# A convolution's kernels loaded with time on the partitions in 64 byte pieces, and the first stage of their transform made from two float16 parts

## The chip, the core and the metric

One core of a Trainium2 chip runs the whole program. The metric is the device time of one execution in microseconds (us). Before the change its median over three runs is 2721.65 us (2719.81 to 2725.82). The engines are named as the profile names them: PE (TensorE, with PEld for its weight loads), ACT (ScalarE), DVE (VectorE), POOL (GpSimd), SP (SyncE, which here only issues DMAs). A queue of an engine runs in the order in which the built program wrote it: an instruction that waits holds back all that stand behind it on that engine.

## What is computed

Four layers follow each other on x of 2048 positions by 640 channels: attention with 32 heads of 20 channels, a convolution over time (S4D), the same attention and the same convolution again. Cut to what matters:

```python
x = x + attention(layernorm(x), wqkv, wo)
x = x + s4d(layernorm(x), ...)        # and both once more, same weights

def s4d(u):
    dt = exp(log_dt); A = -exp(log_A_real) + 1j*A_imag; C = (C_real + 1j*C_imag)*dt[:, None]
    K = 2*einsum("dn,dnl->dl", C, exp((A*dt[:, None])[:, :, None]*arange(L))).real   # 640 x 2048
    y = irfft(rfft(u, 2L) * rfft(K, 2L))[:L]
    return y + u*D_skip
```

K holds one kernel of 2048 taps for each of the 640 channels. Both convolutions use the same K, so the program makes K once, transforms it once, and keeps its transform in HBM.

## The kernel before, in words

**The attention.** For each of 8 groups of heads and 4 blocks of 512 queries the kernel walks over 16 tiles of keys (`attention`, from line 394). `scores` (L824) fills a PSUM tile S, ACT takes its exponential into `pt` (2048 activations of 128 by 1024), and `values` (L841) adds up `pa`, two PSUM tiles with one buffer each. At the end of a block DVE takes `pa` out (`COPY oc<-pa`, then an add of the second tile), and only then can the next block's first `values` write it again. The division by the sum of the exponentials goes by HBM: POOL writes the sums (`dn<-oc`), reads them back (`dr<-dn`), DVE inverts `dr`, POOL writes and spreads it (`db<-dn`), and DVE multiplies one block later. While the attention runs, the object `Plan` estimates when each engine is free, and that decides which pieces of other work stand between the attention's instructions. In this part DVE, ACT, POOL and SP are tied to the order in which the instructions are written down.

**The kernels K.** `kgen` (L182) makes K during the first attention: DVE builds tables of powers, PE contracts them (`contract`, L315), DVE takes the result out as `ko`, and POOL writes `ko` to the HBM tensor `kd`, 640 channels by 2048 taps. Its last piece is written during the last group of heads. Then `end_jobs` calls `prefetch` (L972), which loads `wo`, splits it on POOL, and loads `x` again for the residual.

**The output projection.** `out_proj` (L1092) runs 16 steps `s`. Each takes a tile `otl` of the attention's output from HBM, splits it into `oh` (ACT) and `ol` (DVE), makes 30 matmuls of 128 by 320 into two PSUM tiles `po` (L1098, L1104), and DVE adds them to x. Behind it `ln_u` (L1013) makes the next layernorm: statistics on DVE, `u` on DVE, the float16 part `uh` on ACT and the rest `ul` on POOL.

**The transform of K.** `ktransform` (L1029) is written into step 2 of the first `out_proj`, and the scheduler mixes both. For each of five sets of 128 channels `unit_load` (L1044) does this:

- It loads `kl` from `kd`, with channels on partitions and 8 KB in a row, and adds the skip weight to tap 0 (one DVE instruction of 128 by 1).
- 16 float32 transposes on PE (L1053) turn it into `ktr`, time on partitions. ACT and DVE take them out of PSUM.
- Stage one: 32 float32 matmuls of 128 by 128 with the table `e1` (L1061), into 8 PSUM tiles `pkx` (two buffers), which ACT and DVE take out in turn into `kx`.
- Then 8 steps `q` of a pipeline: four transposes (L1070), ACT takes them out (`kxt`), one float32 matmul of 128 by 512 with `f2` (L1078), two shuffles on DVE into `kn`, one sign product on ACT, and after every second step two DMAs of 512 KB to the HBM tensors `kha` and `khb`.

**The convolution.** `ssm` (L1128) follows. Its `stage1` (L1155) makes, from `uh` and `ul` and a float16 table `e1s` in two parts, three float16 matmuls of 128 by 128 for each one that a float32 form would need (L1163).

Of the kernel before, what the change touches and what calls it, by code (L numbers as in the profile page):

```python
# [11 lines left out]
F32 = mybir.dt.float32  # L12
F32R = mybir.dt.float32r
F16 = mybir.dt.float16
# [70 lines left out]
def mha_s4d_kernel(ctx, tc, x_in, wqkv, wo, lar, aim, cr, ci, ldt, dsk,  # L85
# [23 lines left out]
    def pst(pool, *a, **k):  # L109
        return ps_[pool].tile(*a, **k)  # L110
# [21 lines left out]
    warm = cp.tile([P, 1], F32, name="warm")  # L132
    ve.memset(flag, 0.0)
# [48 lines left out]
    def kgen():  # L182
# [180 lines left out]
        while pend or busy():  # L363
            yield "wait"
        kw2.__exit__(None, None, None)
# [606 lines left out]
    def prefetch(x, rest):  # L972
# [40 lines left out]
    def ln_u(x, i0, n, mvrs, uh, ul, pool):  # L1013
        mv, rs = mvrs
        for i in range(n):
            s = i0 + i
            u = pool.tile([P, D], F32, name="u")
            ve.tensor_scalar(u, x[:, s, :], mv[:, i, 0:1], rs[:, i:i + 1], ALU.subtract, ALU.mult)
            se.copy(uh[:, s, :], u)
            (ve if s == NI - 1 else ge).tensor_sub(ul[:, s, :], u, uh[:, s, :])  # L1020
# [8 lines left out]
    def ktransform():  # L1029
# [4 lines left out]
        e1 = c1.tile([P, NI, 2, P], F32, name="e1")  # L1034
        sy.dma_start(e1, c_e1.rearrange("p (i r k) -> p i r k", i=NI, r=2))
# [5 lines left out]
        skip = c1.tile([P, NCT], F32, name="skip")  # L1041
        sy.dma_start(skip, dsk)

        def unit_load(b):  # L1044
            kl = c1.tile([P, L], F32, name="kl")
            sy.dma_start(kl, kd[b * P:b * P + P, :])
            ve.tensor_add(kl[:, 0:1], kl[:, 0:1], skip[:, b:b + 1])
            kt = c1.tile([P, NI, P], F32, name="ktr")
            klv = kl.rearrange("d (p i) -> d i p", i=NI)
            for i4 in range(4):  # L1050
                pt = pst("T", [P, 4, P], F32, tag="T", name="pkt")
                for i in range(4):
                    te.transpose(pt[:, i, :], klv[:, 4 * i4 + i, :], ident)  # L1053
                (se.copy if i4 % 2 else ve.tensor_copy)(kt[:, 4 * i4:4 * i4 + 4, :], pt)
                yield
            x1 = c1.tile([P, 32, NI // 2, 16], F32, name="kx1")
            for i2 in range(NI // 2):
                ps = pst("X", [P, 2, 2, P], F32, tag="X", name="pkx")
                for r in range(2):
                    for i in range(2):  # L1060
                        te.matmul(ps[:, r, i, :], e1[:, 2 * i2 + i, r, :], kt[:, 2 * i2 + i, :],  # L1061
                                  start=True, stop=True)
                (ve.tensor_copy if i2 % 2 else se.copy)(by_channel(x1, i2), ps.rearrange("p r i (g c) -> p (r i) g c", c=4))
                yield
            prev = None
            for q in range(9):
                if q < 8:
# [4 lines left out]
                    se.copy(xt, pt.rearrange("p g k -> p (g k)"))  # L1072
                if prev is not None:
                    g0 = b * 32 + 4 * (q - 1)
                    if q % 2:
                        kn = [c1.tile([P, 2, 512], F32, name=f"kn{s}") for s in range(2)]
# [270 lines left out]
    def seq(x, general):  # L1347

        stats = None
        for n in range(0, len(parts), 2):  # L1350
            with ExitStack() as c:
# [16 lines left out]
                with ExitStack() as c2:  # L1368
                    up2 = c2.enter_context(tc.tile_pool(name="up2", bufs=2))

                    def ln(i0, m):
                        ln_u(x, i0, m, ln_stats(lambda i: x[:, i0 + i, :], m), uh, ul, up2)
# [3 lines left out]
                    else:  # L1376
                        if n == 0:
                            filler[:] = ktransform(), 0.0, False
# [91 lines left out]
```

## Time and profile before

| What | Time |
|---|---|
| median of three runs | 2721.65 us |
| the profiled execution | 2718.84 us |
| its span, from its first to its last instruction | 2717.1 us |
| granted TensorE clock over the span | 0.991 |
| PE busy | 2534.4 us (93%) |
| ACT busy | 2337.4 us (86%) |
| DVE busy | 1477.0 us (54%) |
| POOL busy | 852.6 us (31%) |
| the first attention's last `pa` taken out of PSUM | 1100.95 us after the start |
| first L1104 matmul of `out_proj` in layer 1 | 1102.4 us |
| first transpose of `ktransform` | 1140.96 us |
| last matmul of `out_proj` in layer 1 | 1282.24 us |
| last `pkf` matmuls of `ktransform` begin | 1277.44 us |

The profile gives busy time for each engine, the idle time before a group of instructions with what ended it, and on request a timeline of any stretch and the sums of a stretch. An average over the span says little here, since in the attention ACT never rests and in the output projection PE hardly does. A stage has to be read by its own rows.

### The profile page before, as it was taken

Reading aid. Unit: us, or ns where it says so; the run is one execution under the profiler, and the core shown is the slowest. Engines: PE = TensorE matmul, PEld = TensorE weight load, DVE = VectorE, ACT = ScalarE, POOL = GpSimd, SP = SyncE. Lnnn points to the kernel's source line nnn. Section 1 sums busy time; section 2 is a strip of 40 time slices with the busy share of each in tenths; the row PEclk is TensorE's granted clock in tenths of the full one; section 3 lists DMA queues with packets and bytes.
Section 4 is the critical chain, followed back from the end, with each engine's and each line's share of the span. In section 5 each row is a group of like instructions: output and inputs, shape, how many; then the busy total and the mean of one; then the engine's idle time right before and its main releaser. Section 6 shows DMA issues by size and latency. Waiting matters only on the chain.

```text
span 2717.1 us, 115609 instructions
## 1 busy us (share of the span) xinstructions
PE 2534.4 (93%) x50944; PEld 1445.2 (53%) x50944; DVE 1477.0 (54%) x3292; ACT 2337.4 (86%) x2762; POOL 852.6 (31%) x1282
## 2 busy tenths in 40 slices
PE   7899999999999988999999999899999998888998
PEld 3445444444444433777886445444445443335988
DVE  7777877778856970577776332232232220003865
ACT  7899999999999999455655899899999999997464
POOL 1132333333333343301670122222223223222376
PEclk9999999999999999999999999999999999999999
DMA  6522222232222232455542111111121112112365
GB/s 214 174 62 75 63 77 64 73 75 61 65 51 59 51 112 87 145 210 194 178 142 67 45 52 52 50 53 46 46 66 35 50 36 61 41 38 80 110 191 161
DMA packets 183153, 238.55 MB, mean 88 GB/s; under 512 B 42737, under 2 KB 128241, under 8 KB 180849
## 3 DMA queue, kind: packets, MB, share of 16 engines
q1 hardware_dynamic: 146304, 184.48, 21.0%
q0 software_dynamic: 36336, 46.59, 7.2%
q8 instruction: 402, 6.59, 1.0%
q14 instruction: 111, 0.90, 0.1%
HBM read 154.90 MB, written 76.03 MB: 85 GB/s over the span
## 4 chain that ended last, share of the span: by engine, by line
ACT 49%; PE 30%; issue 9%; DVE 7%; DMA 4%; POOL 1%; SPq 0%; ACTq 0%; DVEq 0%; POOLq 0%
ACT pt L77 47%; PE pa L841 5%; PE S L824 3%; PE psv L1198 3%; PE po L1104 3%; PE psy L1208 2%; PE m L578 2%; PE psx L1186 2%; PE psx L1163 2%; PE po L1098 1%; PE pst L1173 1%; PE pkf L1078 1%; DMA kop<-ks 1%; PE pv L544 1%; PE pq L730 1%
## 5 line engine op out<-in xcount | busy, mean ns | idle before, releaser
L77 ACT ACTIVATE pt<-S 128x1024 f32<-128x1024 f32 x2048 | 1922.9, 1037 | 46.7 <-PE S L824 37.1
L841 PE MATMUL pa<-pt,V 64*32 64x512 f32 x16384 | 1101.0, 590 | 0.9 <-DVE oc L77 0.8
L824 PE MATMUL S<-qop,kop 61*32 61x512 f16 x16384 | 880.4, 381 | 125.4 <-ACT pt L77 105.1
L824 PEld LDWEIGHTS <-kop 61*32 61x32 f16 x16384 | 375.1, 89 | 784.1 <-issue 660.0
L841 PEld LDWEIGHTS pa<-pt,V 64*32 64x32 f32 x16384 | 315.0, 106 | 69.9 <-DVE oc L77 6.6
L77 POOL DMA_DIRECT2D dn<-oc x256 | 126.7, 501 | 700.9 <-DVE oc L77 644.7
L77 DVE COPY oc<-pa 128x512 f32<-128x512 f32 x64 | 44.2, 690 | 312.1 <-PE pa L841 307.2
L77 DVE TENSOR_SCALAR qc<-m 128x512 f32<-128x512 f32 (+1 forms) x68 | 46.9, 689 | 296.4 <-PE m L578 296.4
L77 POOL DMA_DIRECT2D db<-dn x256 | 130.0, 513 | 111.6 <-DMA dn<-dr 107.7
L578 PE MATMUL m<-xh,wh 64*32 64x512 f16 x2560 | 146.7, 379 | 1.4 <-DVE qc L77 1.4
L578 PE MATMUL m<-xh,wl 64*32 64x512 f16 x2560 | 147.3, 378 | 0.0
L578 PE MATMUL m<-xl,wh 64*32 64x512 f16 x2560 | 145.5, 377 | 0.0
L77 POOL DMA_DIRECT2D ot<-oc x256 | 130.2, 516 | 12.7 <-issue 8.3
L578 PEld LDWEIGHTS <-wh 64*32 64x32 f16 x5120 | 92.5, 94 | 74.1 <-issue 32.6
L1191 POOL TENSOR_TENSOR t<-t,kb 128x512 f32<-128x512 f32 x80 | 102.0, 1276 | 72.3 <-DVE t L77 58.2
L77 ACT COPY xt<-pst 128x1024 f16<-128x1024 f16 x80 | 81.5, 1022 | 47.6 <-PE pst L1173 47.5
L77 POOL DMA_DIRECT2D dn<-dr x64 | 35.8, 559 | 257.5 <-DVE dr L77 237.1
L544 PEld LDWEIGHTS <-xh 128*128 128x128 f16 x960 | 79.6, 98 | 50.9 <-issue 35.6
L77 DVE TENSOR_TENSOR kb<-ktab 128x512 f32<-128x512 f32 x160 | 106.3, 682 | 0.0
L77 DVE TENSOR_SCALAR V<-m 128x160 f32<-128x160 f32 x64 | 20.7, 324 | 156.3 <-PE m L544 156.3
L77 DVE TENSOR_SCALAR dr<-dr 128x16 f32<-128x16 f32 x64 | 11.0, 171 | 171.8 <-DMA dr<-dn 171.6
L1020 POOL TENSOR_TENSOR ul<-u,uh 128x640 f16<-128x640 f32 x30 | 46.1, 1555 | 177.7 <-ACT uh L77 177.7
(269 smaller groups left out, 4045.7 us busy)
## 6 DMA issues: line engine op xcount, KB each, us to landing
ka<-kha SPq DMA_DIRECT2D x80, 256.0 KB
kb<-khb SPq DMA_DIRECT2D x80, 256.0 KB
db<-dn POOLq DMA_DIRECT2D x256, 64.0 KB, 2.7
kpw<-wd POOLq DMA_DIRECT2D x60, 192.0 KB, 4.8
qop<-qs SPq DMA_DIRECT2D x256, 40.0 KB
kop<-ks SPq DMA_DIRECT2D x128, 80.0 KB
ot<-oc POOLq DMA_DIRECT2D x256, 40.0 KB, 2.3
otl<-ot SPq DMA_DIRECT2D x32, 320.0 KB
```

Of the source, the lines that this page charges most:

```text
L77: made = f(out, *a, **k)
L544: chain(te.matmul(ps[:, :n], a_[:, ct, sl], m[:, ct, :], start=(k == 0), stop=(k == 14)))
L578: chain(te.matmul(ps[r][32 * t:32 * t + 32, :], a_[rows, ct, 32 * u:32 * u + 32], m[rows, ct, 512 * v:512 * v + 512], start=(k == 0), stop ...
L824: chain(te.matmul(S[32 * t:32 * t + 32, 512 * r:512 * r + 512], kt_[rows, kc + 32 * t:kc + 32 * t + 32], qt[rows, :], start=True, stop=Tru ...
L841: chain(te.matmul(pa[r][32 * j:32 * j + 32, :], V[rows, kt, VP * h:VP * h + 32], pts[j // 2][rows, 512 * (j % 2):512 * (j % 2) + 512], sta ...
L1020: (ve if s == NI - 1 else ge).tensor_sub(ul[:, s, :], u, uh[:, s, :])
L1104: te.matmul(pos[hf], oh[:, ct, :], m[:, ct, 320 * hf:320 * hf + 320], start=False, stop=(ct == NCT - 1 and m is wol))
L1163: te.matmul(ps[:, r, i, :], e1[:, e, s, r, :], m[:, s, bs], start=(n == 0), stop=(n == 2))
L1186: te.matmul(px, f2[:, f, :], xt[:, k, :], start=(n == 0), stop=(n == 2))
L1191: ge.tensor_mul(t2, t2, kb)
L1198: te.matmul(pv[:, g].rearrange("p r i c -> p (r i c)"), t1[:, g * P:g * P + P], fa, start=True, stop=True)
L1208: te.matmul(py[:, i, :], eb[:, 4 * i4 + i, r, :], v[:, r, 4 * i4 + i].rearrange("p g c -> p (g c)"), start=(r == 0), stop=(r == 1))
```

## The change

- `kgen` gets an end: after its last write DVE takes the largest absolute value of `cr`, `ci` and the skip weights (three reductions), POOL takes the largest over the partitions (`partition_all_reduce`), and seven small DVE instructions make from it two scale factors `ksc`, powers of two.
- `prefetch` makes two buffers `klp_` of 128 by 128 by 16 float32, and appends the loads of the first two sets of channels to the list that is worked off during the last group of heads, behind the loads of x. `load_kl` makes two DMAs for a set. Each takes 64 channels, with the partition as time divided by 16: each piece is 16 taps of one channel, 64 bytes, and one DMA has 128 times 64 = 8192 such pieces.
- In `ktransform` the transposes into `ktr` and their copies go. `parts_of` adds the skip weight (now on one partition, 1 by 128), makes `kth` (ACT, float16, scaled) and `ktl` (DVE, `scalar_tensor_tensor`, the rest in float16), both in two halves of 128 by 1024 that read `kl` with a step of 64 bytes, and then issues the load of the set after next into the same buffer. The parts of the next set are made right after stage one of the present set, ahead of its `q` steps.
- Stage one uses `e1s` of the convolution in place of a float32 table of its own (whose load of 2 MB goes), and three float16 matmuls in place of one float32: 96 for a set. Of the 8 tiles `pkx` DVE takes out 2 and ACT 6, where it was 4 and 4. `kxt` is scaled back while it is copied. `kn` gets two buffers where it had one.
- In the first layer `u` is made on ACT (one activation of 128 by 640 with scale and bias) and no longer on DVE, which makes a small product `nb` instead.

```diff
@@ kgen, after its last contraction
+        for n, t in enumerate((ld["cr"], ld["ci"], skip)):
+            ve.reduce_max(big[:, n:n + 1], t, axis=AX.X, apply_absolute_value=True)
+        ge.partition_all_reduce(most[:, 0:3], big[:, 0:3], P, bass.bass_isa.ReduceOp.max)
...
+        ve.tensor_scalar_mul(ksc[:, 1:2], big[:, 0:1], 2.0 ** -14)
@@ prefetch
+        if rest:
+            klp_[:] = [w1.tile([P, P, NI], F32, name=f"kl{n}") for n in range(2)]
+            rest.extend(lambda b=b: load_kl(b) for b in range(2))
+    def load_kl(b):
+        for h in range(2):
+            d0 = b * P + 64 * h
+            sy.dma_start(klp_[b % 2][:, 64 * h:64 * h + 64, :], kd[d0:d0 + 64, :].rearrange("d (p i) -> p d i", i=NI))
@@ ln_u
+            if on_act:
+                se.activation(u, x[:, s, :], AF.Identity, scale=rs[:, i:i + 1], bias=nb[:, i:i + 1])
@@ ktransform
+        def parts_of(b):
+            kl = klp_[b % 2]
+            sk = c2.tile([1, P], F32, name="sk")
+            sy.dma_start(sk, dsk[:, b:b + 1].rearrange("p o -> o p"))
+            ve.tensor_add(kl[0:1, :, 0], kl[0:1, :, 0], sk)
+            hl = [c1.tile([P, NI, P], F16, name=f"kt{n}") for n in "hl"]
+            klv = kl.rearrange("p d i -> p i d")
+            for h in range(2):
+                sl = slice(8 * h, 8 * h + 8)
+                se.activation(hl[0][:, sl], klv[:, sl], AF.Copy, scale=ksc[:, 0:1])
+                ve.scalar_tensor_tensor(hl[1][:, sl], klv[:, sl], ksc[:, 0:1], hl[0][:, sl], ALU.mult, ALU.subtract)
+            if b + 2 < NCT:
+                load_kl(b + 2)
+            return hl
-                for r in range(2):
-                    for i in range(2):
-                        te.matmul(ps[:, r, i, :], e1[:, 2 * i2 + i, r, :], kt[:, 2 * i2 + i, :],
-                                  start=True, stop=True)
-                (ve.tensor_copy if i2 % 2 else se.copy)(by_channel(x1, i2), ps.rearrange("p r i (g c) -> p (r i) g c", c=4))
+                for i in range(2):
+                    s = 2 * i2 + i
+                    for r in range(2):
+                        for n, (e, m) in enumerate(((0, hi), (0, lo), (1, hi))):
+                            te.matmul(ps[:, r, i, :], e1[:, e, s, r, :], m[:, s, :], start=(n == 0), stop=(n == 2))
+                (ve.tensor_copy if i2 % 4 == 1 else se.copy)(by_channel(x1, i2), ps.rearrange("p r i (g c) -> p (r i) g c", c=4))
                 yield
+            if b + 1 < NCT:
+                kts.append(parts_of(b + 1))
```

**What moves in the order: the last group of heads.** Below is SP's queue during that group, after the change: `x` is the residual, `kl0` and `kl1` are the two buffers of the kernels, `sk` the skip weights of one set, `qop` the queries of a later block. The number behind a name tells buffers apart.

```order
L77 DMA x_24825<-in_x_in 128x2560 x3
L77 DMA kl0_24831<-kd_63 128x64x16 x2
L77 DMA kl1_24832<-kd_63 128x64x16 x2
L77 DMA sk_26637<-in_dsk 1x128x1
L77 DMA sk_26761<-in_dsk 1x128x1
L77 DMA sk_26997<-in_dsk 1x128x1
L77 DMA sk_27233<-in_dsk 1x128x1
L77 DMA qop01_107<-qs_68 40x1x512
```

Before, the `qop` rows came right behind the three loads of x; the third and fourth `sk` now wait until DVE has read the first and the second. On DVE the same stretch read so before, from the inversion of one block's sums (`dr`) to the next block's `pa` being taken out:

```order
L77 TENSOR_TENSOR oc_24154<-oc_24154,db_24581 128x512
L77 TENSOR_SCALAR dr_24876<-dr_24876 128x16
L77 RECIPROCAL dr_24876<-dr_24876 128x16
L77 COPY oc_25394<-pa0_24843 128x512
L77 TENSOR_TENSOR oc_25394<-oc_25394,pa1_24844 128x512
```

and reads so now:

```order
L77 TENSOR_SCALAR dr_24894<-dr_24894 128x16
L77 RECIPROCAL dr_24894<-dr_24894 128x16
L77 TENSOR_TENSOR kl0_24831<-kl0_24831,sk_26637 1x128
L77 TENSOR_TENSOR kl1_24832<-kl1_24832,sk_26761 1x128
L77 COPY oc_25416<-pa0_24861 128x512
L77 TENSOR_TENSOR oc_25416<-oc_25416,pa1_24862 128x512
```

The two additions of the skip weights stand between the inversion and the next block's `COPY oc<-pa`. They wait for the four `kl` loads and two `sk` loads above.

**What moves in the order: the transform.** On DVE, the first set's `q` steps now begin so; `ktl` are the second set's parts, the additions to `kl0` and `kl1` are those for the third and the fourth set, whose loads follow the first and second set's parts:

```order
L77 SCALAR_TENSOR_TENSOR ktl_26765<-kl1_24832,ksc_81,kth_26764 128x1024 x2
L77 TENSOR_TENSOR kl0_24831<-kl0_24831,sk_26997 1x128
L77 STREAM_SHUFFLE kn0_26786<-pkf_26788 128x512
...
L77 STREAM_SHUFFLE kn1_26815<-pkf_26828 128x512
...
L77 SCALAR_TENSOR_TENSOR nb1_27992<-mv_27975,rs_27983 128x2
L77 TENSOR_TENSOR kl1_24832<-kl1_24832,sk_27233 1x128
L77 COPY kx1_26884<-pkx_26899 128x4x32x4
L77 STREAM_SHUFFLE kn0_26842<-pkf_26844 128x512
```

Before, the additions of the skip weights stood there too, between the copies of `kx`, and waited for loads of 8 KB rows. Now the addition for the fourth set stands between the fourth and the fifth of the eight `q` steps of the first set, and the addition for the fifth set stands at the same place in the second set. On SP both loads stand ahead of the DMAs to `kha` and `khb` of the set in whose steps their addition is.

On PE the mix with `out_proj` changes: of its 480 matmuls 240 stood ahead of `ktransform`'s first instruction and 50 between or behind the last two `pkf` pairs. Now 169 stand ahead, about 25 go with each set, and 186 follow the last `pkf`. In the attention's part PE's order is the same as before, and soon after the first convolution begins all engines' orders are the same again, to the end.

More of the change, by code (lines that the diff above doesn't have):

```diff
@@ L1039, in ktransform @@
         sy.dma_start(sgn, c_sg)
[L1041 to L1055 removed]
+        def parts_of(b):
[12 more added lines that the diff above has]
+            return hl
+        kts = [parts_of(0)]
+        def unit_load(b):
+            hi, lo = kts.pop()
             x1 = c1.tile([P, 32, NI // 2, 16], F32, name="kx1")
```

33 lines of the change are left out of this document (24 added, 9 removed).

## Prediction

> **What bounds the kernel now.** I read the page first for the engines, then stretches by time, because the average hides that the program has two kinds of stage. The page has the sums:
>
> ```profile
> PE 2534.4 (93%) x50944; PEld 1445.2 (53%) x50944; DVE 1477.0 (54%) x3292; ACT 2337.4 (86%) x2762; POOL 852.6 (31%) x1282
> ACT 49%; PE 30%; issue 9%; DVE 7%; DMA 4%; POOL 1%; SPq 0%; ACTq 0%; DVEq 0%; POOLq 0%
> ```
>
> Half of the chain that ended last is ACT: the 2048 exponentials. The other stages hang on PE. The change touches both: it puts loads and DVE work into the end of the first attention, and it rewrites the transform of K inside the first output projection. So I looked at the block boundary in the last group of heads, engine by engine (start, duration, engine, instruction):
>
> ```profile
> 1012.26 0.69 DVE L77 COPY oc<-pa 128x512 f32<-128x512 f32 x1 [2.74 <-PE pa L841]
> 1014.68 2.12 SPq L77 DMA_DIRECT2D x<-in_x_in  x3
> 1032.00 0.25 DVE L77 RECIPROCAL dr<-dr 128x16 f32<-128x16 f32 x1
> 1041.73 0.69 DVE L77 COPY oc<-pa 128x512 f32<-128x512 f32 x1 [9.47 <-PE pa L841]
> 1042.52 0.69 DVE L77 TENSOR_TENSOR oc<-oc,pa 128x512 f32<-128x512 f32 x1
> 1043.30 1.05 PE L841 MATMUL pa<-pt,V 64*32 64x512 f32 x16
> 1037.34 12.21 ACT L77 ACTIVATE pt<-S 128x1024 f32<-128x1024 f32 x13
> ```
>
> DVE is done with the old `pa` at 1042.52 + 0.69 = 1043.2, and PE writes the new one at 1043.30. ACT does 13 exponentials in 12.21 us without a gap. PE's queue is in order, so if DVE frees `pa` late, the scores behind that `values` are late as well, and ACT runs dry: **a delay of DVE here is lost one for one.** Before the change DVE had 9.47 us of slack at this place.
>
> In the transform PE is the limit (columns: stretch and length, then busy us and instructions of PE, PEld, DVE, ACT, POOL, then clock, DMA share, GB/s):
>
> ```profile
> 1153.00:1165.00 12.00, 11.99 (x66) 8.35 (x63) 6.94 (x19) 6.58 (x12) 0.00 (x0) 1.00 0.43 165
> 1262.00:1275.00 13.00, 13.00 (x70) 9.40 (x69) 9.82 (x29) 7.42 (x14) 0.00 (x0) 1.00 0.41 163
> ```
>
> PE never rests, DVE and ACT have 25 to 45% left. Work taken from PE counts there, as long as the order gives PE something else to do.
>
> **PE's saving.** The rows of what goes and of the nearest thing that comes:
>
> ```profile
> 1140.96 1.14 PE L1053 MATMUL pkt<-ident,kl 128*128 128x128 f32 x8 [1.21 <-issue]
> 1143.44 7.85 PE L1061 MATMUL pkx<-ktr,e 128*128 128x128 f32 x64
> L1053 PE MATMUL pkt<-ident,kl x80: 270/277/377, 1141.0 to 1250.1; 128*128 128x128 f32 x80
> 1302.40 0.22 PE L1163 MATMUL psx<-uh,e1s 128*128 128x128 f16 x1
> 1303.07 1.11 PE L1198 MATMUL psv<-fa,t 128*128 128x128 f32 x8
> ```
>
> Stage one's 320 records go at 7.85/64 = 0.123 us: 39.2 us. The 80 transposes go at the same pace: (1.14 - 0.28)/7 = 0.123, 9.8 us. The convolution's stage one ran 12 float16 matmuls from 1302.40 to 1303.07, 0.056 us each, so the new 480 take 26.8 us. PE is relieved of 39.2 + 9.8 - 26.8 = **22.2 us**. Not all of it becomes time, since the order changes too.
>
> **The transform's new chain.** Prices on the other engines:
>
> ```profile
> L77 ACT ACTIVATE wv<-b0s 128x800 f16<-128x800 f32 x2 | 1.8, 886 | 0.2 <-DMA b0s<-in_wqkv 0.2
> L77 ACT ACTIVATE xr<-xr,nb,rs 128x640 f32<-128x640 f32 x16 | 14.0, 925 | 3.0 <-DVE nb L77 2.9
> L77 DVE SCALAR_TENSOR_TENSOR vl<-ws,vh 128x800 f16<-128x800 f32 x4 | 4.0, 994 | 0.1
> L1070 PE MATMUL pkt<-ident,kx x160: 272/273/329, 1152.2 to 1268.8; 128*128 128x128 f32 x160
> L77 ACT COPY kxt<-pkt 128x512 f32<-128x512 f32 x40 | 22.6, 581 | 15.8 <-PE pkt L1070 14.5 <-PE pkf L1078 1.2
> L77 ACT ACTIVATE kn<-kn,sgn 128x512 f32<-128x512 f32 x40 | 27.8, 721 | 17.3 <-DVE kn L77 16.9
> L1104 PE MATMUL po<-woh,oh x320: 302/309/712, 1102.4 to 2558.5; 128*128 128x320 f32 x160
> 1154.87 1.02 PE L1078 MATMUL pkf<-kxt,f 128*128 128x512 f32 x2
> 1156.16 1.08 PE L1078 MATMUL pkf<-kxt,f 128*128 128x512 f32 x2
> 1157.52 1.03 PE L1078 MATMUL pkf<-kxt,f 128*128 128x512 f32 x2
> 2549.94 1.63 PE L1098 MATMUL po<-woh,ol 128*128 128x320 f32 x10
> 2554.34 1.63 PE L1098 MATMUL po<-woh,ol 128*128 128x320 f32 x10
> ```
>
> A half of `kth` is 1024 elements a partition. From 886 ns for 800, about 1 ns for each more, it is 1.11 us, and a scale from memory adds about 0.15 (the 925 ns of `xr` against some 730 that the 800 would scale to): 1.25 us. A half of `ktl` is 994 + 224 = 1.2 us. `u` on ACT is 0.93 us, hidden, since ACT has room; DVE is relieved of the same work. None of these rows reads with a step of 64 bytes; PE's transposes of `kl` did (277 ns at the median, and 273 with no step), so I take the step as free. Its bounds are nothing and a doubling.
>
> One `q` step takes 1.29 and 1.36 us between those `pkf`, and PE, ACT (0.58 + 0.72) and DVE (two shuffles) are all near that, so I keep 1.35. One `out_proj` matmul alone takes 4.40/30 = 0.147 us in the second layer. Now one set, counted from the end of its stage one: 0.9 us to take out the last tile, two `kth` to 3.4, `kxt` to 4.0, first `pkf` at 4.9 (a few `out_proj` matmuls stand ahead of it), eight steps to 15.7, then the 79 matmuls that are left of the next stage one (4.4) and 16 of `out_proj` (2.4): **22.5 us a set.** It starts after 169 `out_proj` matmuls and not 240: 1102.4 + 169/240 of (1140.96 - 1102.4) = 1129.6. First stage one 6.9, four sets more 90, the last steps 15.7: 1242.2. Then 186 matmuls alone, 27.3 us, and 1 us for waits on the two `po` buffers: last at 1270.5.
>
> ```profile
> 1282.24 0.31 PE L1104 MATMUL po<-wol,oh 128*128 128x320 f32 x1
> 1286.93 1.63 DVE L77 TENSOR_SCALAR u<-x,mv,rs 128x640 f32<-128x640 f32 x1
> 1290.83 0.27 PE L1163 MATMUL psx<-uh,e1s 128*128 128x128 f16 x1 [5.04 <-DVE x L77]
> 1296.96 0.39 PE L1173 MATMUL pst<-id,x 128*128 128x128 f16 x4
> ```
>
> Before, the last was done at 1282.5: **12.0 us gained**. The passage into the convolution took 14.4 us more, to 1296.96, with PE waiting 5.04 us, since DVE's last parts of `x` stood behind the whole last layernorm. In the new order most of them stand ahead of it, and `u` is no longer 1.63 us on DVE. The chain from the last `out_proj` matmul is then some 6.2 us of small steps, 0.7 us of matmuls, and 1.5 for what I can't see: 8.4. **Another 6 us gained.** So far 18 us.
>
> **The price of 64 byte pieces.** No row has such a DMA. The nearest are pieces of 128 bytes (32 columns of `wqkv`), when the second layer starts, and the loads of `kpw`, also 128 bytes:
>
> ```profile
> DMA packets 552, 0.15 MB, mean 278 GB/s; under 512 B 426, under 2 KB 551, under 8 KB 551
> DMA to landing us min/median/max: 3.9/4.8/6.7
> dr<-dn POOLq DMA_DIRECT2D x64, 8.0 KB, 2.7
> 1022.00:1026.00 4.00, 3.31 (x80) 1.54 (x87) 0.00 (x0) 4.00 (x5) 0.77 (x2) 1.00 1.01 400
> 1026.00:1030.00 4.00, 3.31 (x88) 1.28 (x65) 0.00 (x0) 4.00 (x5) 0.73 (x2) 1.00 0.41 149
> ```
>
> The first row is a stretch of 0.55 us (1440.45 to 1441.0): 16 engines moved 552 packets, 426 of them 128 bytes. The other 126 carry some 95 KB; at the 400 GB/s of the x loads, 25 bytes a ns on each engine, they take 30 ns each. That leaves (8.8 - 3.8)/426 = 11.7 ns for a small piece. Halving it with the bytes gives 6 ns. `kpw` (second row, 96 pieces an engine) lands 4.8 us after its issue, where 8 pieces land after 2.7: 2.1/88 = 24 ns. I take **11 ns a piece on each engine**, next to the saturated row, and keep 6 and 24. A set has 16384 pieces, 1024 an engine: 11.3 us, where 1 MB in 8 KB rows at 400 GB/s is 2.6.
>
> **First wait, in the attention.** SP issues both `kl` sets behind the three loads of x, which end at 1026 + 0.41 x 4 = 1027.6. Two sets take 2048 x 11 ns = 22.5 us, and 2.7 us until they count as landed (the row of `dr`): 1052.8. DVE meets the additions at 1032, right behind the inversion, and stands. Then 0.3 us for them and 1.5 for `COPY` and add: `pa` is free at 1054.6, not 1043.2. **11.4 us lost.** Behind the waiting addition stand only that copy and what follows it; behind the copy wait PE, and behind PE ACT. The `qop` loads that SP holds back meanwhile are for a block some 14 us later, so they cost nothing. The new end of `kgen` (two reductions, POOL's maximum, seven small steps) ends about 1 us after the block boundary at 1012 had its copy: 1 us more.
>
> **Second wait, in the transform.** The third set's load is issued early enough. The fourth's is issued when the second's `ktl` is done, 4.7 us after stage one, and lands 4.7 + 11.3 + 2.7 = 18.7 us after it. DVE meets its addition after four `q` steps, at 10.3. That is 8.4 us of standing, with shuffles, `pkf` and the PE order behind it; the same in the next set: **16.8 us lost.** The writes of `kha` and `khb` wait behind the same load on SP's queue, until about the same moment, and two `kn` buffers last just that long, so this adds nothing.
>
> The Trainium skill says ("DMA: Bandwidth & Descriptors", "Queues, rings and completion order") that each DMA engine takes the descriptors of one ring in order. By that the first `kha` write could not pass the load ahead of it even with the addition elsewhere; if the engines shared their time between both, that write would cost 1.3 us more and only DVE's place would count. No run here shows which.
>
> **Sum.** -12.0 - 6 + 16.8 + 12.4 = +11.2 on the profiled execution of 2718.84 (span 2717.1 and 1.7 around it): 2730.0. The median, 2721.65, is 2.8 above that execution; I let the forecast stand at 2730 us, 0.3% over the median. Rounds of this kernel can tell about 0.2% from no change.
>
> **The rivals.**
>
> *Hidden loads* (the other side). If a piece costs 6 ns or less, the attention's wait falls to 1.2 us, the transform's to two of 3.2, and with the 1 us of `kgen` the sum is -18 + 8.6 = -9.4; with better mixing than my 22.5 us a set, -16. About 2703 to 2710, 2706 in the middle. It decides at 5.4 ns: there both sets land before 1043. For it speaks that bytes halve; against it that the saturated row at 128 bytes is already twice as slow per byte as long rows, so what is paid is paid by the piece. Chance 0.2.
>
> *Dear pieces.* At 24 ns the attention waits 2048 x 24 ns - 11.1 = 38 us, the transform 2 x 21.7 and some 13 more, as the fourth set's load queues behind the third's: 38 + 1 + 56 - 18 = +77, 2796 us; at 18 ns some 2765. For it speaks `kpw`; against it that `kpw` was no saturated stream. Chance 0.15. The Trainium skill ("DMA: Bandwidth & Descriptors", "Rules for kernel authors") calls a copy that transposes by its access pattern 19 times slower than the transposing DMA; taken against the 2.6 us above a set would need about 50 us, an estimate beyond even this rival, and the 11.7 ns at 128 bytes speak against it.
>
> *The step costs.* If ACT and DVE read a step of 64 bytes at half speed, each set's steps start 2.5 us later: 12.5 us more, 2742. The Trainium skill ("SBUF — State Buffer", "Door 1: The DMA port swizzle") says that reads which leave a 16 byte line each time pay. PE's 277 against 273 ns speaks against a large price, but on another engine. Chance 0.15.
>
> **How the numbers follow.** The forecast case keeps 0.5, from 2720 to 2742 by a piece of 9.5 to 13 ns and 2 us a set. The range reaches from 2703, through hidden loads, to 2770, which leaves out most of the dear pieces and little else. Faster than 0.2% is nearly all of the hidden loads and a little of the forecast: 0.21. Within 0.2%: 0.15. Slower: 0.64.
>
> **What would show it.** In the profile after: DVE idle before `kl<-kl,sk` with a DMA as its end, some 20 us long near 1032, and a hole in ACT's exponentials of 10 to 13 us behind it; two such waits of 6 to 10 us in the transform; stage one at 0.056 us a matmul; the last `out_proj` matmul 12 us nearer to its first if the two waits are taken off; PE's 5 us hole before the convolution gone. A landing before 1043 makes the prediction wrong on the fast side; `kth` over 2 us, or sets without waits that still take 25, on the slow side.

## The result, and the profile after

The changed kernel takes 2744.26 us (median of four runs, 2741.25 to 2746.57), the kernel before 2721.03 on the same chips: a ratio of 1.0083, 95% interval 1.0067 to 1.0099, or **23 us slower**. The forecast was 2730, the range 2703 to 2770. The profiled execution of the changed kernel has a span of 2744.7 us, 27.6 more than that of before.

First the end of the first attention, the timeline of the changed kernel (start, duration, engine, instruction, and in brackets the idle time ahead of it and what ended that):

```profile
1018.51 28.73 SPq L77 DMA_DIRECT2D kl<-kd  x4
1047.36 10.80 SPq L77 DMA_DIRECT2D sk<-in_dsk  x4
1042.23 0.25 DVE L77 RECIPROCAL dr<-dr 128x16 f32<-128x16 f32 x1
1056.62 0.63 DVE L77 TENSOR_TENSOR kl<-kl,sk 1x128 f32<-1x128 f32 x2 [14.13 <-DMA sk<-in_dsk]
1057.17 0.67 DVE L77 COPY oc<-pa 128x512 f32<-128x512 f32 x1
1057.89 2.72 PE L857 MATMUL pa<-pt,V 64*32 64x512 f32 x16 [16.22 <-DVE oc L77]
1061.17 1.02 ACT L77 ACTIVATE pt<-S 128x1024 f32<-128x1024 f32 x1 [18.12 <-PE S L840]
```

This is the chain that the prediction described: DVE stands at the additions, the copy of `pa` behind them comes at 1057.17, PE waits 16.22 us for it and ACT has 18.12 us without an exponential. What ends DVE's wait is `sk`, which stands behind both sets of `kl` in SP's queue. The block before takes 30.2 us (30.6 before the change), the next one 31.7 and the last 29.8, where each of these blocks took 29.5 before the change. From the copy at 1012.26 to the one at 1100.95 the attention took 88.7 us before the change; the same two copies now stand at 1010.48 and 1118.57, 108.1 us: **19.4 us lost**.

Then the transform, by groups (duration in ns at minimum, median and maximum, then the first and the last start) and by DVE's timeline:

```profile
L77 ACT ACTIVATE kth<-kl,ksc x10: 2028/2060/2076, 1145.2 to 1245.2; 128x1024 f16<-128x1024 f32 x10
L77 DVE SCALAR_TENSOR_TENSOR ktl<-kl,ksc,kth x10: 1975/1990/2028, 1147.2 to 1247.3; 128x1024 f16<-128x1024 f32 x10
1165.25 0.38 DVE L77 TENSOR_TENSOR kl<-kl,sk 1x128 f32<-1x128 f32 x1 [2.53 <-DMA kl<-kd]
1179.17 0.36 DVE L77 TENSOR_TENSOR kl<-kl,sk 1x128 f32<-1x128 f32 x1 [5.33 <-DMA kl<-kd]
1208.83 0.37 DVE L77 TENSOR_TENSOR kl<-kl,sk 1x128 f32<-1x128 f32 x1 [7.90 <-DMA kl<-kd]
L1142 PE MATMUL po<-wol,oh x160: 303/309/616, 1120.2 to 1307.6; 128*128 128x320 f32 x160
```

A half of `kth` or `ktl` costs 2 us and not 1.2, and DVE stands 15.8 us at three additions. From its first L1142 matmul (1120.05) to its last (1307.56) the output projection takes 187.5 us (before: L1104, 1102.43 to 1282.24, 179.8): **7.7 us lost**.

The price of the pieces, from a stretch in which little but one set was moved (DMA statistics from 1152.2 to 1163.9):

```profile
DMA packets 16324, 1.06 MB, mean 91 GB/s; under 512 B 16323, under 2 KB 16323, under 8 KB 16323
1028.00:1053.00 25.00, 10.82 (x232) 4.29 (x216) 0.43 (x2) 15.05 (x17) 9.70 (x17) 0.82 1.39 103
```

16324 pieces on 16 engines in 11.7 us are **11.5 ns a piece on each engine**. The second row is the stretch in which both sets of the attention were loaded. It is a row of sums: stretch and length, then busy us and instructions of PE, PEld, DVE, ACT, POOL, then clock, DMA share and GB/s. For 25 us the DMA share was 1.39, above one, while only 103 GB/s were moved.

Last the passage into the convolution and the rest:

```profile
1307.71 0.23 PE L1201 MATMUL psx<-uh,e1s 128*128 128x128 f16 x1
1313.47 0.22 PE L1201 MATMUL psx<-uh,e1s 128*128 128x128 f16 x1 [1.36 <-DVE lt L77]
L1211 PE MATMUL pst<-id,x x640: 218/219/311, 1318.9 to 2721.1; 128*128 128x128 f16 x160
```

The first `pst` comes 11.3 us after the last L1142 matmul (14.7 before), and PE's longest wait there is 1.36 us in place of 5.04: **3.4 us gained**. From the first `pst` to the end are 1425.8 us, 5.7 more than before, with the same instructions. Of that, 2.5 us arise in one block of the second attention, in which PE waits 2.89 us for the queries and not 1.46; the rest is spread over the blocks behind it. The profiled executions of the other kernels below with the changed transform have 1418.0 to 1425.2 there, and kn_one, which differs from the changed kernel by one buffer, has 1419.4. So I put it down to the execution and not to the change; a cause was not found. Without it the two profiles differ by 22 us, close to the 23 of the medians.

### The profile page after: what moved, and what is told of

Same layout as the page of the kernel before. It is cut to its first block, busy times and chain, and to the rows that moved or that the text cites. A ratio compares the mean times of both kernels' runs of the same rounds, so it can differ in the third digit from the quotient of the medians.

```text
span 2744.7 us, 115805 instructions
## 1 busy us (share of the span) xinstructions
PE 2525.9 (92%) x51024; PEld 1431.8 (52%) x51024; DVE 1478.3 (54%) x3285; ACT 2371.6 (86%) x2788; POOL 852.6 (31%) x1283
## 4 chain that ended last, share of the span: by engine, by line
ACT 49%; PE 28%; issue 9%; DVE 6%; DMA 5%; SPq 1%; POOL 1%; ACTq 0%; DVEq 0%; POOLq 0%
ACT pt L77 46%; PE pa L857 5%; PE S L840 3%; PE psv L1236 3%; PE psy L1246 3%; PE po L1142 2%; PE m L594 2%; PE psx L1224 2%; PE psx L1201 2%; SPq L77 1%; DMA kop<-ks 1%; PE pst L1211 1%; PE po L1136 1%; DMA kl<-kd 1%; PE pv L560 1%
## 5 line engine op out<-in xcount | busy, mean ns | idle before, releaser
L857 PEld LDWEIGHTS pa<-pt,V 64*32 64x32 f32 x16384 | 317.4, 106 | 88.2 <-DVE oc L77 23.4
L1229 POOL TENSOR_TENSOR t<-t,kb 128x512 f32<-128x512 f32 x80 | 101.8, 1273 | 69.2 <-DVE t L77 54.9
```

Of the source, the lines that this page charges most:

```text
L857: chain(te.matmul(pa[r][32 * j:32 * j + 32, :], V[rows, kt, VP * h:VP * h + 32], pts[j // 2][rows, 512 * (j % 2):512 * (j % 2) + 512], sta ...
L1229: ge.tensor_mul(t2, t2, kb)
```

## The experiments

Ratios are to the kernel before on the same chip, with their 95% interval; the changed kernel has 1.0083. "From first `po` to first `pst`" is the stretch from the first `po` matmul of layer 1 to the first `pst`, in the profiled execution: 196.1 us before (1100.9 to 1296.96), 200.4 in the changed kernel.

**late_adds: the first two additions can't stand in the attention.**

```diff
+            if b < 2:
+                ve.scalar_tensor_tensor(sk, x[0:1, 0, 0:P], 0.0, sk, ALU.mult, ALU.add)
             ve.tensor_add(kl[0:1, :, 0], kl[0:1, :, 0], sk)
```

> The changed kernel with one edit: the skip additions of the first two sets take their weights from a tile that is only ready after the first step of out_proj, so that they can't stand in the last group of heads. Loads, pieces and everything else stay. Theory A, the loss in the attention comes from DVE standing before those two additions with the next block's copy behind them: the 18.1 us hole of ACT near 1043 goes, the last pa is taken out at 1099 to 1101 and not at 1118.6, and the whole is 17 to 19 us shorter than the changed kernel, 2725 to 2728 us. Rival B, the 64 byte loads themselves cost the time, since they fill the DMA engines for 25 us and hold SP's queue: the hole moves to the inversion's reload or to the queries, and less than half comes back, 2735 us or more. Both leave the transform as it was, some 7.5 us longer than before the change.

Measured: 2729.03 us, ratio 1.0025 (1.0014 to 1.0035), some 16 us less than the changed kernel. ACT's and DVE's timelines, and what DVE still waits for at `kl` (us, times):

```profile
1043.26 0.69 DVE L77 COPY oc<-pa 128x512 f32<-128x512 f32 x1
1046.21 32.48 ACT L77 ACTIVATE pt<-S 128x1024 f32<-128x1024 f32 x35 [1.05 <-PE S L840]
  DMA kl<-kd: 15.7, 3
```

The hole of 18 us is down to 1.05, though the same pieces fill the same DMA engines. The attention's loss came from where DVE stood: theory A. The transform keeps its 15.7 us of waits.

**long_rows: the same bytes in long pieces.**

```diff
-            sy.dma_start(klp_[b % 2][:, 64 * h:64 * h + 64, :], kd[d0:d0 + 64, :].rearrange("d (p i) -> p d i", i=NI))
+            sy.dma_start(klp_[b % 2][64 * h:64 * h + 64], kd[d0:d0 + 64, :].rearrange("p (d i) -> p d i", i=NI))
```

> The changed kernel with the same bytes loaded into kl in the same order, but each row of 8 KB whole, so in long pieces; kl then holds other numbers, with channels on partitions, and the transform works on those. Theory A, the price of the small pieces is all that was lost, through the waits behind it: no hole in the attention (18 us back) and none of the 15.8 us of waits for kl in the transform; with the follow-on of these, 30 to 36 us shorter than the changed kernel, 2708 to 2714 us, and faster than before the change by 7 to 13 us. Rival C, the transform was bound by its new order and by the slow making of kth and ktl, and the waits for kl only stand in front of that: only the attention's part comes back, 2724 to 2728 us.

Measured: 2715.13 us, ratio 0.9970 (0.9956 to 0.9985), some 31 us less than the changed kernel: theory A. SP's queue, ACT at the block boundary, and two stretches of the transform (PE, PEld, DVE, ACT, POOL, then clock, DMA share, GB/s):

```profile
1017.61 3.25 SPq L77 DMA_DIRECT2D kl<-kd  x4
1047.22 1.02 ACT L77 ACTIVATE pt<-S 128x1024 f32<-128x1024 f32 x1 [3.82 <-PE S L840]
1152.00:1180.00 28.00, 26.30 (x206) 18.93 (x205) 22.47 (x58) 24.86 (x36) 2.81 (x2) 1.00 0.76 244
```

SP hands the four loads over in 3.25 us where it needed 28.73. The clock stays at 1.00 in the transform; in the changed kernel it falls behind each wait:

```profile
1164.00:1180.00 16.00, 9.99 (x62) 6.75 (x61) 8.06 (x26) 8.97 (x14) 1.40 (x1) 0.89 1.27 140
1180.00:1191.00 11.00, 10.08 (x86) 8.48 (x86) 8.14 (x23) 7.23 (x11) 1.41 (x1) 0.84 0.78 305
1209.00:1222.00 13.00, 11.39 (x93) 10.02 (x93) 8.63 (x22) 7.74 (x10) 0.00 (x0) 0.79 0.73 284
```

From first `po` to first `pst` it takes 182.9 us, 17.5 less than the changed kernel: nearly all of the 15.8 us of waits (1.0 us is left) and some of the slow clock. But a hole of 3.82 us is left in the attention, with no 64 byte piece anywhere. early_scales takes that up.

**no_step: neighbours read in place of a step of 64 bytes.**

```diff
-            klv = kl.rearrange("p d i -> p i d")
+            klv = kl.rearrange("p d i -> p (d i)").rearrange("p (i d) -> p i d", i=NI)
```

> The changed kernel, but kth and ktl read kl without the step of 64 bytes, 1024 neighbouring numbers for a half; the numbers that they read are then other ones. Loads and waits stay. Theory S, the step is what makes a half cost 2.06 us on ACT and 1.99 on DVE: they fall to about 1.25 and 1.2, and since two halves of ACT and one of DVE stand on each set's path, 2.4 us a set come back, 10 to 12 us in all, 2732 to 2735 us. Rival T, the duration is that of the kind of instruction and not of the step: both stay near 2 us and the time near 2744. Rival U, the halves get shorter but PE has out_proj to do meanwhile: 2740 to 2744 us.

Measured: 2737.04 us, ratio 1.0049 (1.0033 to 1.0064), some 9 us less than the changed kernel: theory S, a little under its size.

```profile
L77 ACT ACTIVATE kth<-kl,ksc x10: 1134/1146/1157, 1144.3 to 1239.0; 128x1024 f16<-128x1024 f32 x10
L77 DVE SCALAR_TENSOR_TENSOR ktl<-kl,ksc,kth x10: 1264/1280/1285, 1145.5 to 1240.4; 128x1024 f16<-128x1024 f32 x10
```

The waits for `kl` stay (15.1 us). The step alone costs 0.91 us a half on ACT and 0.71 on DVE.

**u_on_act: before, with only `u` moved to ACT.** The edit is the change's own in `ln_u`, shown above.

> The kernel before with only one part of the change: in the first layer u is made on ACT. Theory P, the passage into the convolution is shortened by the 1.63 us of u and what stood behind it on DVE: 2 to 4 us less than before, 2717 to 2719 us, with PE's hole of 5 us before stage one cut to 1 to 2. Rival Q, the passage only becomes shorter with the new order of the transform, which ends earlier: within 1 us of before, 2720 to 2722.

Measured: 2717.99 us, ratio 0.9979 (0.9969 to 0.9989), 3 to 8 us less than before. But the hole that theory P wanted to cut is still there:

```profile
1290.97 0.27 PE L1169 MATMUL psx<-uh,e1s 128*128 128x128 f16 x1 [5.17 <-DVE x L77]
L1179 PE MATMUL pst<-id,x x640: 216/219/314, 1296.7 to 2692.7; 128*128 128x128 f16 x160
```

In the profiled execution the passage is 13.8 us (14.7 before), and the stretch from first `po` to first `pst` 194.1, 2 us less. So the time agrees with theory P and the mechanism doesn't: with `u` on ACT alone the hole of 5 us stays. It is gone in the changed kernel, which has `u` on ACT and the new order of the transform; the new order with `u` on DVE was not run. Why the medians show more than those 2 us is open.

**f16_rows: the change without its small pieces.** Whole rows and 16 transposes a set as before, float16 parts made from PSUM, everything else as changed.

```diff
+            kl = c1.tile([P, L], F32, name="kl")
+            sy.dma_start(kl, kd[b * P:b * P + P, :])
...
+                    te.transpose(pt[:, i, :], klv[:, 4 * i4 + i, :], ident)
+                se.activation(hi[:, sl], pt, AF.Copy, scale=ksc[:, 0:1])
+                ve.scalar_tensor_tensor(lo[:, sl], pt, ksc[:, 0:1], hi[:, sl], ALU.mult, ALU.subtract)
```

> The changed kernel without its 64 byte loads: each set is loaded in whole rows inside the transform and turned by 16 transposes, as before the change; ACT and DVE make kth and ktl straight from the transposes' PSUM tiles. Float16 stage one, u on ACT, the two kn buffers and the scales stay. Theory A, what the change lost it lost by the loads and by the step with which kl is read, and the rest of it gains: PE is relieved of 12.4 us of stage one, u on ACT gave 5 us alone, together 2704 to 2710 us. Rival R, the transform hangs on its chain of small steps and not on PE's work, so that float16 alone gives nothing: 2715 to 2719, what u on ACT alone gave.

Measured: 2707.07 us, ratio 0.9964 (0.9953 to 0.9976): theory A. The transposes that the change took out cost PE 9.8 us, and putting them back, which does away with the small pieces, the waits for them and the step, is worth 32 us. From first `po` to first `pst` it takes 181.8 us, 14.3 less than before.

**three_buffers: all small pieces, no addition early.**

```diff
-            klp_[:] = [w1.tile([P, P, NI], F32, name=f"kl{n}") for n in range(2)]
+            klp_[:] = [w1.tile([P, P, NI], F32, name=f"kl{n}") for n in range(3)]
...
+            ve.scalar_tensor_tensor(sk3, after, 0.0, sk3, ALU.mult, ALU.add)
...
-                        kn = [c2.tile([P, 2, 512], F32, name=f"kn{s}") for s in range(2)]
+                        kn = [(c1, c2)[s].tile([P, 2, 512], F32, name=f"kn{s}") for s in range(2)]
```

> The changed kernel with all its 64 byte loads, but no DVE instruction waits for one: kl gets three buffers, the first three sets are loaded in the last group of heads, and each skip addition hangs on a tile that is ready shortly before it is needed (out_proj's first x, then the set before's kx), so that it can't be put early. To make room kn0 has one buffer and kn1 two. Theory A, the pieces cost only through the additions that wait for them: beside the attention's hole the 15.7 us of waits in the transform go, and the half clock behind them: 2706 to 2713 us, like the kernel with long rows. Rival B, 16384 pieces a set fill the DMA engines and SP's queue, and three sets in the attention delay the queries and the sums of the next blocks: the attention loses 5 us or more, and the writes of kha and khb wait behind the later sets: 2722 us or more.

Measured: 2730.16 us, ratio 1.0047 (1.0030 to 1.0064): rival B. No addition waits any more, and two other instructions do:

```profile
1048.03 0.18 DVE L77 TENSOR_SCALAR dr<-dr 128x16 f32<-128x16 f32 x1 [35.72 <-DMA dr<-dn]
1158.70 6.57 SPq L77 DMA_DIRECT2D kl<-kd  x2
1165.37 6.03 SPq L77 DMA_DIRECT2D kha<-kn  x1
1175.62 0.01 DVE L77 LOAD_MASK_SELECT kn<-pkf  x1 [11.27 <-DMA kha<-kn]
```

In the attention the inversion of `dr` stands ahead of the copy of `pa`, and its 8 KB come 16 us later than before the change (1031.79). Most of that delay is not the pieces' doing, since long_rows, which has none, shows the same instruction 10 us late:

```profile
1042.20 0.17 DVE L77 TENSOR_SCALAR dr<-dr 128x16 f32<-128x16 f32 x1 [29.84 <-DMA dr<-dn]
```

The three blocks take 101.8 us here (1010.23 to 1112.04), 93.9 in long_rows and 88.7 before the change. So of 13.1 us lost about 8 go beyond long_rows and are put down to the three sets of pieces; early_scales takes up the rest. In the transform the shuffle into `kn` waits for a write that stands behind the load in SP's queue. These waits sum to 16.2 us, where the additions' were 15.8: the wait has moved and hardly shrunk, with 195.2 us from first `po` to first `pst`. But the tile that the write empties, `kn0`, has only one buffer in this kernel. How much of the wait two buffers would bridge was not run.

**writes_on_act: the writes on another queue.**

```diff
-                            sy.dma_start(dst[:, g0 - 4:g0 + 4, :].rearrange("p g k -> p (g k)"),
+                            se.dma_start(dst[:, g0 - 4:g0 + 4, :].rearrange("p g k -> p (g k)"),
```

> The kernel with three buffers, but the writes of kha and khb are issued by ACT on a queue of its own, so that no load of kl stands ahead of them in a queue; the DMA engines are the same. Theory O, it is the order in SP's queue that holds the writes back: DVE's wait of 11.3 us for kha goes to 3 or less, and the whole is 6 to 12 us shorter than three_buffers, 2718 to 2724. Rival E, it is the engines, full of small pieces, that hold them back: the wait stays at 8 us or more, and with 40 issues more on ACT the time is that of three_buffers or longer, 2728 to 2735.

Measured: 2757.97 us, ratio 1.0152 (1.0133 to 1.0172). Neither theory's time came. ACT's and DVE's timelines and the waits:

```profile
1157.95 0.35 ACTq L77 DMA_DIRECT2D kha<-kn  x1
1163.97 0.01 DVE L77 LOAD_MASK_SELECT kn<-pkf  x1 [4.39 <-DMA kha<-kn]
DVE kn L77 <- DMA kha<-kn: 20.7, 10, 4.4
ACT kn L77 <- DVE kn L77: 46.3, 34, 4.9
```

On its own queue the first write lands 6 us after its issue with a load under way, and DVE waits 4.39 us and no longer 11.27. So most of the long wait was SP's queue, in which the write was only reached at 1165.37. Whether the shared engines cause what is left is not shown: with one buffer and no small piece, before the change, DVE waited for these writes too:

```profile
DVE kn L77 <- DMA kha<-kn: 8.8, 6, 2.2
```

But ACT issues in order too: it now waits 46 us for DVE's `kn` (13.9 with three buffers), and DVE for `kha` ten times. From first `po` to first `pst` it takes 223.8 us, 28.6 more than three_buffers. That ACT's waits with one `kn0` are the reason is argued; ACT's queue with two buffers was not run.

**step_on_pe: the step given to PE.**

```diff
-                se.activation(hl[0][:, sl], klv[:, sl], AF.Copy, scale=ksc[:, 0:1])
+                se.activation(hl[0][:, sl], kl[:, sl], AF.Copy, scale=ksc[:, 0:1])
...
-                            te.matmul(ps[:, r, i, :], e1[:, e, s, r, :], m[:, s, :], start=(n == 0), stop=(n == 2))
+                            te.matmul(ps[:, r, i, :], e1[:, e, s, r, :], m[:, :, s], start=(n == 0), stop=(n == 2))
```

> The kernel with three buffers, and kth and ktl written in the order of kl, so that ACT and DVE read and write neighbours and PE reads its moving operand with a step of 32 bytes. Theory S, the step costs ACT and DVE time but not PE: a half falls from 2.06 and 1.99 us to 1.15 and 1.28, stage one stays at 0.056 us a matmul, and 6 to 10 us come off the kernel with three buffers. Rival V, PE pays for the step: stage one's 480 matmuls go from 0.056 to 0.08 or more, 12 us or more on PE, and nothing is gained or the time grows.

Measured: 2809.20 us, ratio 1.0339 (1.0322 to 1.0356), 79 us more than three_buffers: rival V, and far beyond its size.

```profile
1153.16 0.41 PE L1099 MATMUL pkx<-ktl,e1s 128*128 128x128 f16 x1
1153.40 0.65 PE L1099 MATMUL pkx<-kth,e1s 128*128 128x128 f16 x2
1153.86 0.41 PE L1099 MATMUL pkx<-ktl,e1s 128*128 128x128 f16 x1
1150.00:1160.00 10.00, 10.00 (x45) 5.43 (x44) 3.10 (x12) 1.86 (x4) 0.00 (x0) 0.50 1.12 65
1212.19 0.41 PE L1099 MATMUL pkx<-ktl,e1s 128*128 128x128 f16 x1
1212.89 0.41 PE L1099 MATMUL pkx<-ktl,e1s 128*128 128x128 f16 x1
1212.00:1216.00 4.00, 4.00 (x19) 2.05 (x18) 1.90 (x6) 0.72 (x1) 0.00 (x0) 1.00 0.32 131
```

Three matmuls in 0.70 us are 0.233 each, four times the 0.056 of neighbours. The pace is the same where the granted clock is 0.50 and where it is 1.00, so here the step sets it and not the clock. The clock, in turn, stood at 0.50 from 1150 to 1160 although PE was busy for all of these 10 us. The extra time of the 480 matmuls is 480 x 0.177 = 85 us, next to 79 for the whole kernel; what ACT and DVE save and what the lower clock costs the other matmuls was not separated.

**kn_one: one `kn` buffer, as before the change.**

```diff
-                        kn = [c2.tile([P, 2, 512], F32, name=f"kn{s}") for s in range(2)]
+                        kn = [c1.tile([P, 2, 512], F32, name=f"kn{s}") for s in range(2)]
```

> The changed kernel with one buffer for each kn, as before the change. Theory K, SP's queue holds the writes of kha and khb behind the loads of kl, and two buffers just bridge that: with one, DVE waits at every second q step of the third and fourth set, 8 to 20 us more than the changed kernel, 2752 to 2764. Rival L, DVE already stands at its additions until the load has landed, so that the writes are not what it waits for: 2743 to 2748.

Measured: 2738.39 us, ratio 1.0078 (1.0061 to 1.0095), the same as the changed kernel: rival L.

```profile
DVE kl L77 <- DMA kl<-kd: 11.2, 3, 5.9
DVE kn L77 <- DMA kha<-kn: 7.3, 3, 3.1
```

The waits are exchanged: less for the load (15.8 in the changed kernel), more for `kha` (1.5 there).

**early_scales, on f16_rows: the scale factors made early.** The block of the diff's first part stands right behind the factor of `cr` and `ci` in `kgen`, and no longer at its end.

> The kernel of f16_rows, and the scale factors ksc are made early in kgen, right after cr and ci have got their factor, and no longer at its end in the last group of heads. Theory G, the maximum over the partitions on POOL at kgen's end is followed by about 9 us in which POOL does nothing, so that the sums of the next block (dn, dr) come late, DVE's inversion stands ahead of the copy of pa, and ACT has a hole of 3 us near 1040: it goes, the blocks take 29.5 us each as before the change, 3 to 5 us less than f16_rows. Rival H, that idle stretch of POOL comes before the first wol product anyway, as in the kernel before the change: within 1 us of f16_rows.

> The kernel of f16_rows once more, on the same chip as early_scales, as its base: 0.9964 of the kernel before, give or take 0.0012.

Measured on one chip: early_scales 2702.90 us, ratio 0.9950 (0.9934 to 0.9967); f16_rows_again 2705.86, ratio 0.9957 (0.9942 to 0.9972). The intervals overlap, so the profiles have to decide. POOL and ACT in f16_rows:

```profile
1006.13 0.37 POOL L77 PARTITION_ALL_REDUCE kmost<-kbig  x1 [0.39 <-DVE kbig L77]
1022.41 1.54 POOL L1005 TENSOR_TENSOR wol<-wot,woh 128x640 fp32r<-128x640 f32 x1 [9.96 <-issue]
1032.59 1.69 POOL L77 DMA_DIRECT2D dn<-oc  x3
1043.62 1.02 ACT L77 ACTIVATE pt<-S 128x1024 f32<-128x1024 f32 x1 [3.34 <-PE S L840]
```

and in early_scales:

```profile
1001.36 1.54 POOL L1005 TENSOR_TENSOR wol<-wot,woh 128x640 fp32r<-128x640 f32 x1 [8.63 <-issue]
1015.31 1.95 POOL L77 DMA_DIRECT2D dn<-oc  x4
999.41 71.44 ACT L77 ACTIVATE pt<-S 128x1024 f32<-128x1024 f32 x77
```

ACT has no hole, and the same three blocks take 88.7 us (1008.78 to 1097.46) as before the change, where f16_rows_again has 92.6 (1007.95 to 1100.52): 3.9 us. POOL's idle 9 us stand before its first `wol` product in both, so rival H has the origin right; but with `kgen`'s late end they stand in the way of the block's sums, so theory G has the effect and the size. This version has the lowest median of all, **0.5% faster than before** (0.3 to 0.7), with the change's float16 stage one and without its loads.

## Why the prediction was right, and where it was off

The sign and the place were right; the forecast of +9 us was some 14 short of the 23. A piece cost 11.5 ns, inside the 9.5 to 13 that the prediction gave its own case, but the time lies just above that case's 2720 to 2742: what fell short were other terms. Step by step, in the profiled executions:

- **The price of a piece**: 11 ns forecast, 11.5 measured where a set is alone. *Hidden loads* and *dear pieces* fall by that row.
- **First wait**: 11.4 us forecast, 17.2 measured at the copy and 2.2 more one block later. The mechanism is shown (late_adds). The size failed in two ways. The landing was put at 1052.8: the pieces took 25 us and not 22.5, beside the attention's own small DMAs, and DVE waits for `sk`, which lands last, until 1056.6. And the copy would have been due at 1040, since the blocks ran 1.8 us earlier. In the next block PE starts at half the pace: 16 `values` took 2.72 us behind the hole, 1.05 before the change.
- **The end of `kgen`**: 1 us forecast, for the small steps on DVE; those cost about 0.3 us, ACT's gap of 0.26 us behind them. What it costs is POOL's idle time in another place, 3.9 us in f16_rows. In the changed kernel the longer wait covers it.
- **PE's saving and a set's chain**: 12.0 us of gain forecast before waits. long_rows, which has 1.0 us of such waits in the transform, has its last L1142 matmul 169.9 us after its first, against 179.8: 9.9 us. Stage one ran at 0.056 us a matmul as forecast. **The step was taken as free**, on the matmul rows of PE's transposes of `kl`. Those rows name the streamed tile first and the weights second, as `pkx<-kth,e1s` does, where the code streams `kth`: it is the weight load that reads `kl`, and its rows, below, show 196 ns with the step and 141 without. no_step shows that a half of `kth` takes 2.06 us on ACT with the step and 1.15 without, and that the step costs the kernel 9 us. The Trainium skill's sentence on reads that leave a 16 byte line ("SBUF — State Buffer", "Door 1: The DMA port swizzle") agrees with 2.06 against 1.15 us. These 9 us are the rival *The step costs*, which had 12.5, and its sign, `kth` over 2 us, came. It adds to the forecast's case and does not replace it. That the forecast of a set was close is in part luck: 22.5 us without a price for the step, where the parts `kth` of long_rows' second to fifth set begin 23.4, 22.5 and 23.2 us apart with the step in them. The rest of the chain was shorter than forecast by most of what the step adds.
- **Second wait**: 16.8 us forecast at two additions, 15.8 measured at three. "Issued early enough" failed for the third set, which lost 2.5 us. What I left out is that PE runs slower behind each of them (0.89, 0.84 and 0.79 above). The Trainium skill says ("TensorE: Matmul & The Clock Gate", "Part 1: The HAM clock gate") that the clock is set by how busy PE has been; these rows agree. The 0.50 of step_on_pe, with PE busy throughout, shows that the profile's busy time alone does not tell the clock.
- **Rather the queue than DVE's place**: I had left open whether the writes would pass the load. three_buffers shows that in one queue they don't (11.27 us), writes_on_act that on another they do (4.39 us). The rule of the Trainium skill that the prediction cites there ("DMA: Bandwidth & Descriptors", "Queues, rings and completion order"), each ring in order, agrees with both. But in three_buffers SP was also held by handing over the load, for 6.57 us, before it came to the write, and the two were not told apart. Moving the additions alone did not bring back the 16 us of the transform, in a kernel with one `kn0`.
- **Two `kn` buffers**: the prediction let the held-back writes add nothing because of them. With one buffer the time is the same (kn_one), so they were not needed for that.
- **The passage**: 6 us forecast, 3.4 measured. PE's hole went, as forecast, but the passage still took 11.3 us and not 8.4. `u` on ACT does not remove the hole by itself (u_on_act); that the new order does is likely, but was not run without `u` on ACT.
- **Queries held back in SP's queue cost nothing**: no run tried this by itself. late_adds, with SP held as long, has 1.2 us more than before in these three blocks.

The weight loads of the transposes before the change, of `kl` with the step and of `kx` without:

```profile
L1053 PEld LDWEIGHTS pkt<-ident,kl x80: 185/196/210, 1140.9 to 1250.0; 128*128 128x128 f32 x80
L1070 PEld LDWEIGHTS pkt<-ident,kx x160: 137/141/145, 1152.1 to 1268.6; 128*128 128x128 f32 x160
```

The sum of the terms: +19.4 in the attention, -1.8 because its last three blocks began 1.8 us earlier, +7.7 in the output projection, -3.4 in the passage, and the 5.7 behind it, 27.6 for a difference of spans of 27.6. The forecast had 11.2 for the same difference. Of the 16.4 us between them, the attention makes 5.2 (17.6 against 12.4), the output projection 2.9 (7.7 against 4.8), the passage 2.6 and the unexplained 5.7 the rest. So the forecast term that was mis-sized most is the attention's.

## What to carry to other kernels

A load in 64 byte pieces is priced by the piece: 11.5 ns on each engine, hardly less than the 11.7 that the prediction worked out for 128 bytes. So 1 MB takes 11.7 us where long rows would take some 2.6, an estimate from the 400 GB/s of the x loads; before one uses it to save a set's 16 transposes, their 2 us of PE stand against 9 us of a full queue. It costs most by who waits: a tiny instruction on its data, put early in an in-order queue, stops an engine that a saturated one depends on. When that instruction was moved here, the next transfer in the same queue took over the wait. Give such an addition a dependence that is ready just before its use, and look at what else the load's queue carries.

## What the runs showed of the hardware

- SP itself is held while it hands over small pieces: 28.73 us for four DMAs of 8192 pieces, 3.25 for the same bytes in rows. What stands behind in its queue starts later by that: the first `sk` load was issued at 1047.36, right behind them.
- A float16 moving operand with a step of 32 bytes runs at 0.233 us a matmul of 128 columns, at a granted clock of 0.50 and of 1.00 alike, with neighbours at 0.056. A float32 weight load of 128 by 128 for a transpose took 196 ns with a step of 64 bytes and 141 with neighbours.
- ACT and DVE pay for a step of 64 bytes with 0.91 and 0.71 us per 1024 float32 a partition.
- Holes of PE of 2.85, 3.34 and 5.49 us in the transform lie in or before stretches with a granted clock of 0.89, 0.84 and 0.79, where long_rows, without them, has 1.00. Under the stepped matmuls of step_on_pe the clock was 0.50 for 10 us without a hole.
